# A fused adaLN attention and gated-MLP block: one chunk's output projection in two parts, one more quad off ScalarE, order constants anew

## The chip, the cores and the metric

One core of a Trainium2 chip runs the whole kernel in one launch. The metric is the device time of that launch in microseconds. The kernel before takes 805.92 us (median of three runs, 805.61 to 806.03).

Five engines run side by side, each through its own instruction stream, in order: PE (TensorE, matmuls), DVE (VectorE), ACT (ScalarE), POOL (GpSimd) and SP (SyncE, which here issues nearly all DMAs). They meet through semaphores.

## What is computed

```python
def _A_ref(x, wqkv, wo):                      # B, S, D = 1, 2048, 640; 32 heads of 20
    qkv = (x @ wqkv).reshape(B, S, 3, H, Dh).transpose(2, 0, 3, 1, 4)
    q, k, v = qkv
    p = softmax(einsum('bhqd,bhkd->bhqk', q, k) * Dh ** -0.5)
    o = einsum('bhqk,bhkd->bhqd', p, v)
    return o.transpose(0, 2, 1, 3).reshape(B, S, D) @ wo

def _B_ref(x, w_gate, w_up, w_down):          # F = 1536
    return ((x @ w_gate) * (x @ w_up)) @ w_down

sa, ca, ga, sb, cb, gb = (silu(c) @ w_mod).reshape(1, 6, 1, 640)   # six vectors
x = x + ga * _A_ref(layernorm(x) * (1 + ca) + sa, A_wqkv, A_wo)
x = x + gb * _B_ref(layernorm(x) * (1 + cb) + sb, B_w_gate, B_w_up, B_w_down)
```

All arrays are bf16. The layer norms have no weights of their own.

## The kernel before

**Tiling.** The 2048 query rows are cut into five chunks (`CHUNKS`): three of 512 rows and two of 256. The 32 heads are eight sets of four, numbered 0 to 7; the four heads of a set lie in the four 32-row strips of the PE array. An *item* is one head set of one chunk, 40 in all, and they run one after the other. For an item the scores of all 2048 keys are computed in units of 512 columns (one key tile by 512 queries, or two key tiles by 256 queries), 64 units in an item of the first three chunks and 32 in one of the last two.

**Two ways to the exponential.** Most units go in pairs into two PSUM banks, and ACT takes the exponential of 128x1024 in one instruction (line 1530). There are two such pairs of banks, used in turn, so a pair's next score matmuls wait until ACT has read it. The other units go to DVE in *quads* of four units: line 1554 turns each unit's scores into 16-bit integers in a buffer `DB`, lines 1586 and 1594 split their bits into a mantissa and an exponent part, and a product of the two parts (line 1591 on DVE, or four pieces at line 1646 on POOL) gives a first term; the exponent part is the second term. Both are multiplied with V, so a unit in a quad takes two PV matmuls where one on ACT takes one. `QUADS` gives the number of quads of each item, 109 in all.

**PV and the end of an item.** `pv_issue` (line 2179) multiplies the probabilities with V, accumulating in one PSUM bank. At the end of an item (`item_end_tasks`) DVE transposes the sums to `OT` (t1, line 1724), takes reciprocals of the row sums (t2, line 1728), POOL scales (t3, line 1730), DVE transposes back into one of two `OcT` buffers (t4, line 1738), and SP copies the rows with small DMAs into `Ocp` (line 1751), in which the rows of all heads lie packed as the output projection needs them. For set 7 of the last chunk alone (`direct`) there is no such DMA: the last row block of `Ocp` is zeroed at that chunk's set 0 (`z_tail`, line 1719), and the projection adds a sixth pass that reads `OcT` itself against `wo7`, a copy of the last 80 rows of `wo` laid out in the strips of `OcT`.

**After a chunk.** `suffix(ci)` makes the work that follows: the rows of x are loaded into `xck` by one DMA (line 1857); 8 rounds (4 row tiles by 2 column halves of 320; 4 rounds in the last two chunks) project `Ocp` with `wo` in five passes of 128 rows, and DVE adds x in `xck` (line 1878); statistics (1892, 1894, 1895, 1897) and the normalization into `xn2` (1900); transposes to `h2T` (1914, 1921); 12 blocks of gate and up with weights that SP streams into `stg`, or `stx` for the last two chunks (lines 951 and 947 on PE); the down projection from `hprod`; and the store. All chunks but the last do this while the next chunk's attention runs, in the places that the scores leave free on PE. Each round has a *gate*: it may not start before a number of exponentials have been issued. The last chunk's suffix comes after the last exponential, together with what is left of the fourth chunk's.

**What sets the order.** Nothing is reordered on the chip. At build time a planner (`Sched`) plays through all tasks with costs in nanoseconds, priorities and gates, and writes down the order on each engine; `emit_program` then adds the semaphore waits. On PE, `pick_pe` takes the next score matmuls when their banks are free, with up to two units of a quad attached; otherwise it takes PV work, or a round of the projections, or, where recent activity is low and nothing else is ready, a *zero fill* (`zero_fill`, line 2546: four matmuls that add zero into the PV bank). How it chooses depends on some fifteen constants, which `STAGE` sets for each item: how early a quad's units may be attached (`EAGER`) or must be (`D_LATE`, `D_RES`), how late scores may become through other work (`X_LATE`, `PVTOL`, `HOLD`), how much PV work is taken at once, from what activity on to fill (`FILL_MIN`, `FILL_Z`), and priorities of the products.

**Rounds and banks.** A `Round` is a group of matmuls into one PSUM bank with an evacuation. Rounds and quads' units share three banks (`G`). A round's first matmul waits for all its inputs, and since PE is in order, so does everything behind it. The out-projection of a chunk before the last waits for all DMAs into `Ocp` of its eight sets (`oc_ready`).

Of the kernel before, what the change touches and what calls it, by code (L numbers as in the profile page):

```python
# [329 lines left out]
def emit_program(nc, sched, nsem_dma=56):  # L330
# [97 lines left out]
    with nc.Block() as block:  # L428
# [20 lines left out]
        def _(e):  # L449
# [10 lines left out]
HALF = [0, 0, 4, 0, 0]  # L460
RESID, RES_G = 1, -20
D_LEAD = 0.451
# [80 lines left out]
    3: {"STEAL_GAP": 200, "PVMAX": 5, "FILL_MIN": 3892.39, "PVTOL": 199, "XBACK": 3, "D_RES": 11, "EAGER": 7, "D_LATE": 10},  # L543
    4: {"XBACK": 1, "PVMAX": 9, "EAGER": 3, "PVTOL": 324, "D_RES": 23, "Z_LATE": 272.45, "FILL_Z": 3546.61},
    5: {"EAGER": 7, "D_RES": 18, "PVCAP": 6, "FILL_MIN": 3318.38, "PVMIN": 1, "PVTOL": 124, "HOLD": 185, "FILL_Z": 4642.7, "D_LATE": 22, "STEAL_GAP": 244.44},
    6: {"PVCAP": 12, "FILL_MIN": 4293.4, "D_LATE": 12, "PVMIN": 5, "EAGER": 9, "TPRIO": 0.87, "HOLD": 80, "XDPRIO": 2.63, "FILL_Z": 3011.56},
    7: {"DL": 0.501, "PVTOL": 347, "D_LATE": 18, "HOLD": 155, "PVMAX": 9, "EAGER": 4, "X_LATE": 18.5},
    8: {"PVCAP": 15, "PVMAX": 3, "Z_LATE": 19.94, "FILL_Z": 3656.07, "FILL_MIN": 4663.83, "TPRIO": 0.57, "EAGER": 16, "PVMIN": 1, "XBACK": 3, "STEAL_GAP": 194.45, "XDPRIO": 2.05},
    9: {"X_LATE": -14.35, "PVCAP": 12, "XBACK": 0, "HOLD": 65, "PVMIN": 3, "D_LATE": 24, "PVMAX": 6, "D_RES": 23, "FILL_MIN": 4103.55, "XDPRIO": 1.63, "PVTOL": 224},
    10: {"PVMAX": 9, "X_LATE": -27.967, "EAGER": 5, "D_LATE": 15, "PVCAP": 8, "XBACK": 0, "HOLD": 110, "FILL_Z": 3693.44, "Z_LATE": -95.95, "PVMIN": 2, "XDPRIO": 1.25, "PVTOL": 199, "D_RES": 17},  # L550
    11: {"DL": 0.443, "X_LATE": 54.31, "FILL_MIN": 4086.76, "PVTOL": 270, "PVMAX": 6, "PVCAP": 14, "D_LATE": 22, "Z_LATE": -74.79, "EAGER": 4},
    12: {"DL": 0.459, "D_LATE": 11, "STEAL_GAP": 194.93, "X_LATE": -138.337, "HOLD": 125, "FILL_Z": 3256.59, "PVMIN": 1, "D_RES": 29},
    13: {"DL": 0.417, "D_RES": 4, "HOLD": 99, "PVMAX": 4, "TPRIO": 0.51, "PVMIN": 5, "STEAL_GAP": 145.61, "PVCAP": 13, "FILL_MIN": 5235.75, "FILL_Z": 2424.75, "PVTOL": 324, "Z_LATE": -67.84, "XDPRIO": 1.14},
    14: {"D_LATE": 14, "D_RES": 16, "FILL_MIN": 4279.59, "EAGER": 11, "X_LATE": -150.94, "STEAL_GAP": 200, "PVTOL": 374, "FILL_Z": 3396.29, "HOLD": 50, "XDPRIO": 1.59, "PVMAX": 10, "TPRIO": 1.17, "PVCAP": 9},
    15: {"X_LATE": -189.21, "EAGER": 15, "Z_LATE": -100, "D_RES": 5, "HOLD": 65, "PVMAX": 4, "PVMIN": 4, "PVTOL": 199, "STEAL_GAP": 191.33, "D_LATE": 14},
    16: {"D_RES": 67, "HOLD": 88, "PVCAP": 11, "PVMIN": 3, "PVTOL": 299, "STEAL_GAP": 83.35, "EAGER": 7, "Z_LATE": 121.81, "FILL_MIN": 4640.79, "FILL_Z": 2909.17, "D_LATE": 20, "X_LATE": 34.41, "PVMAX": 8, "XBACK": 1},
    17: {"D_LATE": 23, "PVMAX": 10, "PVMIN": 5, "FILL_MIN": 4231.45, "EAGER": 4, "FILL_Z": 3806.89, "PVCAP": 9, "XBACK": 4, "Z_LATE": 101.76, "TPRIO": 1.29, "HOLD": 80},
# [37 lines left out]
def build_kernel(nc, A_x, A_wqkv, A_wo, B_x, B_w_gate, B_w_up, B_w_down, c, w_mod, out):  # L595
# [195 lines left out]
    def dve(dur, f, deps=(), prio=3.0, **k):  # L791
        return sc.add(Task("dve", dur, f, deps, prio=prio, **k))
# [1829 lines left out]
```

## Time and profile before

| | |
|---|---|
| median of three runs | 805.92 us |
| the profiled execution | 805.69 us |
| its span, first to last instruction | 803.8 us |
| first exponential (line 1530) starts | 15.9 us |
| last exponential starts | 765.9 us |
| exponentials | 806 |
| quads (lines 1586 and 1594 each) | 109 |
| zero fills (line 2546) | 328 matmuls, in sets of four |
| products on POOL (line 1646) and on DVE (line 1591) | 264 pieces, 43 whole |

The page of the profile gives busy time, the span in 40 slices, the chain of work that ended last, and groups of instructions: line, engine, operation, output<-input, shapes, count | busy us, mean ns of one | idle time of the engine before them, and what ended it. A view of windows gives each engine's busy time (and instruction count) in a stretch, then the granted clock of PE, the DMA share and GB/s. A view of waits gives the waiting instruction, what it waited for, us in total, times and the longest. The timeline gives start, length, engine, line, operation and count; in it a run of matmuls ends with the modelled end of its last one, so that its neighbour's start tells more. For one line there is a view with the minimum, median and maximum duration, and the first and last start.

The output projection of the third chunk (512 rows, items 16 to 23) starts at 587.0 us on PE, and the first score matmuls of the fourth chunk at 575.5 us.

### The profile page before, as it was taken

How to read it: one execution, taken by the hardware profiler on the slowest of the kernel's cores; microseconds unless marked ns; L12 is line 12 of the kernel's file. 1: busy time of each engine (PE TensorE's matmuls, PEld its weight loads, DVE VectorE, ACT ScalarE, POOL GpSimd, SP SyncE). 2: the span in 40 equal slices, each digit the busy share in tenths (PEclk: the TensorE clock that was granted, in tenths of full speed). 3: DMA queues.
4: the chain of work that ended last, by engine and by line, in shares of the span. 5: the costliest groups of instructions: out<-in, count | busy, mean ns of one | idle time of the engine just before them, and what ended most of it. 6: DMA issues, size and time to landing. Idle time of an engine off the chain costs nothing.

```text
span 803.8 us, 29783 instructions
## 1 busy us (share of the span) xinstructions
PE 790.9 (98%) x12801; PEld 306.6 (38%) x12801; DVE 693.3 (86%) x1283; ACT 762.1 (95%) x851; POOL 364.1 (45%) x370
## 2 busy tenths in 40 slices
PE   8999999999999999999999999999999999999998
PEld 4433333222233223233233333333245544454577
DVE  7979977999989899989998999999689867978963
ACT  7899999999999999999999999999999999999922
POOL 3303266365665452156456553454475435443610
PEclk9999999999999999999999999999999999999999
DMA  9634211114330225000301221000303353004110
GB/s 311 208 87 109 68 46 40 44 37 126 87 73 23 58 66 173 18 15 23 95 7 24 54 56 34 5 23 23 87 9 71 82 131 86 13 24 105 31 38 17
DMA packets 108577, 52.80 MB, mean 66 GB/s; under 512 B 76043, under 2 KB 108447, under 8 KB 108447
## 3 DMA queue, kind: packets, MB, share of 16 engines
q1 hardware_dynamic: 107519, 49.75, 23.6%
q8 instruction: 102, 1.67, 0.9%
q10 hardware_dynamic: 928, 1.15, 0.4%
q14 instruction: 28, 0.23, 0.1%
HBM read 39.88 MB, written 8.41 MB: 60 GB/s over the span
## 4 chain that ended last, share of the span: by engine, by line
PE 61%; ACT 31%; DVE 4%; issue 3%; DMA 1%; ACTq 0%; DVEq 0%
ACT PP L1530 30%; PE ps_all L1492 20%; PE ps_all L951 20%; PE ps_all L2179 14%; PE ps_all L947 3%; DVE DB L1554 1%; PE ps_all L2546 1%; PE ps_all L1211 1%; DMA wm<-in_w_mod_dram 1%; PE ps_all L1914 1%; PE ps_all L1147 1%; PE ps_all L1108 1%; DVE wd L1475 1%; DVE DSS L1586 0%; DVE DSS L1594 0%
## 5 line engine op out<-in xcount | busy, mean ns | idle before, releaser
L1530 ACT ACTIVATE PP<-ps_all 128x1024 bf16<-128x1024 f32 x806 | 742.2, 1136 | 3.9 <-PE ps_all L1492 3.0
L1646 POOL TENSOR_TENSOR DSS<-DB,DSS 128x512 bf16<-128x512 bf16 x264 | 300.3, 1158 | 321.7 <-DVE DSS L1594 275.1
L1554 DVE TENSOR_SCALAR DB<-ps_all 128x512 int16<-128x512 f32 x436 | 290.3, 683 | 57.5 <-PE ps_all L1492 54.5
L1492 PE MATMUL ps_all<-QT,KT 32*128 32x512 bf16 (+1 forms) x2560 | 314.0, 340 | 7.1 <-ACT PP L1530 4.9
L1492 PEld LDWEIGHTS ps_all<-QT,KT 32*128 32x128 bf16 x2560 | 81.7, 91 | 263.2 <-ACT PP L1530 224.6
L2179 PE MATMUL ps_all<-PP,Vf 128*32 128x512 bf16 (+1 forms) x2024 | 159.1, 344 | 0.0
L951 PE MATMUL ps_all<-h2T,stg 128*32 128x512 bf16 (+2 forms) x1912 | 117.7, 329 | 0.0
L2179 PE MATMUL ps_all<-DSS,Vf 128*32 128x512 bf16 (+3 forms) x1072 | 85.1, 343 | 0.3 <-DVE DSS L1594 0.2
L1594 DVE TENSOR_SCALAR DSS<-DB 128x2048 int16<-128x2048 int16 x109 | 77.5, 711 | 1.3 <-PE ps_all L2179 1.2
L1586 DVE TENSOR_SCALAR DSS<-DB 128x2048 int16<-128x2048 int16 x109 | 74.9, 687 | 0.3
L2179 PEld LDWEIGHTS ps_all<-PP,Vf 128*32 128x32 bf16 x2024 | 44.6, 94 | 80.3 <-issue 75.3
L1730 POOL TENSOR_TENSOR OTn<-OT,invT 128x512 bf16<-128x512 f32 (+1 forms) x39 | 37.2, 953 | 53.5 <-DVE invT L1728 53.5
L951 PE MATMUL ps_all<-wd,hprod 128*32 128x320 bf16 (+1 forms) x1332 | 60.1, 283 | 0.2 <-DVE xck L2060 0.2
L951 PEld LDWEIGHTS ps_all<-h2T,stg 128*32 128x32 bf16 x1912 | 41.4, 95 | 31.1 <-issue 22.2
L1591 DVE TENSOR_TENSOR DSS<-DB,DSS 128x2048 bf16<-128x2048 bf16 x43 | 53.1, 1236 | 0.1
L951 PEld LDWEIGHTS ps_all<-wd,hprod 128*32 128x32 bf16 x1332 | 29.3, 96 | 19.3 <-issue 11.5
L2179 PEld LDWEIGHTS ps_all<-DSS,Vf 128*32 128x32 bf16 (+1 forms) x1072 | 26.6, 95 | 20.8 <-issue 11.9
L951 PE MATMUL ps_all<-wV,hT 128*32 128x320 bf16 (+1 forms) x696 | 32.5, 290 | 0.0
L1211 PE MATMUL ps_all<-hT,wq 128*32 128x512 bf16 x375 | 31.4, 383 | 0.2
L951 PE MATMUL ps_all<-wo,Ocp 128*32 128x320 bf16 (+1 forms) x660 | 29.9, 281 | 0.1
L2546 PE MATMUL ps_all<-ident 128*32 128x512 bf16 x328 | 29.0, 383 | 0.0
L1724 DVE STREAM_TRANSPOSE OT<-ps_all 128x512 f32<-128x512 f32 (+1 forms) x40 | 24.1, 603 | 5.3 <-PE ps_all L2179 5.3
(130 smaller groups left out, 529.8 us busy)
## 6 DMA issues: line engine op xcount, KB each, us to landing
stg<-in_B_w_gate_dram SPq DMA_DIRECT2D x44, 160.0 KB, 3.9
stg<-in_B_w_up_dram SPq DMA_DIRECT2D x44, 160.0 KB
QT<-q_rows SPq DMA_DIRECT2D x22, 128.0 KB, 2.5
KT<-k_rows SPq DMA_DIRECT2D x84, 32.0 KB, 2.9
wm<-in_w_mod_dram SPq DMA_DIRECT2D x3, 800.0 KB
x<-in_A_x_dram SPq DMA_DIRECT2D x7, 320.0 KB
xck<-in_A_x_dram SPq DMA_DIRECT2D x3, 640.0 KB, 4.6
wd<-in_B_w_down_dram SPq DMA_DIRECT2D x1, 1920.0 KB
```

What stands on the lines that cost most here:

```text
L951: return lambda e, b: e.matmul(ps[32 * x:32 * x + 32, b, c0 + o:c0 + o + w], lhs()[:, 32 * x:32 * x + 32], rhs() if w == n else rhs()[:, o ...
L1211: f = [lambda e, b_, k=k, x=x: e.matmul(ps[x:x + min(32, w - x), b_, :], wx[:, k, r0 + x:r0 + min(x + 32, w)], hT[tc][:, k, :], tile_posit ...
L1492: ems.append(lambda e, i=i, kt=kt: e.matmul(dstf()[:, i * u.n:(i + 1) * u.n], KT[32 * u.s:32 * u.s + 32, u.j, kt * 128:(kt + 1) * 128], QT ...
L1530: return e.activation(PPs[g % 2][:, cellp["p"], 0:nu * 512], ps[:, b0:b0 + nu, :].rearrange("p b c -> p (b c)"), AFT.Exp, scale=ESCALE)
L1554: return e.tensor_scalar(DBl[st_["slot"]][:, x * 512:(x + 1) * 512], bank(cell["b"]), EBIAS, 0.0, op0=ALU.add, op1=ALU.max)
L1586: return e.tensor_scalar(DSl[st_["ss"][0]][:, :], DBl[st_["slot"]][:, :], 0x7F, 0x3F00, op0=ALU.bitwise_and, op1=ALU.bitwise_or)
L1591: return e.tensor_tensor(d, DBl[st_["slot"]][:, :].bitcast(BF16), d, ALU.mult)
L1594: return e.tensor_scalar(DSl[st_["ss"][1]][:, :], DBl[st_["slot"]][:, :], 0x7F80, 2, op0=ALU.bitwise_and, op1=ALU.bitwise_or)
L1646: return e.tensor_tensor(d, DBl[st_["slot"]][:, x * w:x * w + w].bitcast(BF16), d, ALU.mult)
L1730: f3 = lambda e: e.tensor_tensor(OTn[:, 0:n].rearrange("p (b c r) -> p b r c", c=32, r=2), OT[:, 0:n].rearrange("p (b r c) -> p b r c", c= ...
L2179: ems.append(lambda e, i=i, kt=kt, stt=stt, stp=stp: e.matmul(ps[32 * s:32 * s + mc, BPV, 0:u.n], Vf[:, (kt * H + 4 * u.j + s) * VW:(kt * ...
L2546: task.emits = [lambda e, x=x: e.matmul(ps[32 * x:32 * x + 32, b_, :].rearrange("p (a b) -> p a b", a=4), ident[:, 32 * x:32 * x + 32], id ...
```

## The change

`QUADS` gets one quad more, in set 6 of the fourth chunk: 110.

For the third chunk (`OPA_C = (2,)`) set 7 is now `direct` as in the last chunk: no DMAs into `Ocp`, and the row block is zeroed at that chunk's set 0. Its out-projection is made in two parts. Eight rounds `oa` take the five passes over `Ocp` without waiting for set 7, with a gate 30 exponentials before the next chunk, and their evacuation adds x and writes an fp32 buffer `pf`. Eight rounds `op` then take the one pass over `OcT` with `wo7`, and their evacuation adds `pf` and writes `xck`. `pf` lies where `h2T` and `xn2` lie; so the evacuations into it wait for the chunk before to be done with `h2T`, and the normalization into `xn2` waits for the second part's evacuations of tiles 2 and 3. x is loaded a tile at a time, each tile after the store of that tile of the chunk before. Priorities on DVE and POOL are given for these tasks (`OPA_P`, `OPB_P`, `OPL_P`, `OPX_P`).

The constants in `STAGE` are replaced for 36 of the 40 items (3 to 10 and 12 to 39).

```diff
-         (1, 2, 1, 2, 2, 1, 1, 2),
+         (1, 2, 1, 2, 2, 1, 2, 2),
          (1, 2, 2, 1, 3, 0, 2, 2))
 HALF = [0, 0, 4, 0, 0]
 RESID, RES_G = 1, -20
+OPA_C, OPA_G, OPB_G, OPA_P, OPB_P, OPL_P, OPX_P = (2,), -30, 0, 0.7, 0.6, 0.6, 0.6
...
-    3: {"STEAL_GAP": 200, "PVMAX": 5, "FILL_MIN": 3892.39, "PVTOL": 199, "XBACK": 3, "D_RES": 11, "EAGER": 7, "D_LATE": 10},
+    3: {"STEAL_GAP": 200, "PVMAX": 5, "FILL_MIN": 3892.39, "PVTOL": 199, "XBACK": 3, "D_RES": 11, "EAGER": 6, "D_LATE": 10},
...
-    22: {"PVMAX": 4, "FILL_MIN": 2500, "D_RES": 17, "EAGER": 6, "D_LATE": 14, "PVCAP": 10, "PVTOL": 224, "STEAL_GAP": 189.38, "FILL_Z": 4191.54, "HOLD": 200, "X_LATE": -70.46, "PVMIN": 4},
+    22: {"PVMAX": 4, "FILL_MIN": 2500, "D_RES": 11, "EAGER": 6, "PVCAP": 13, "PVTOL": 224, "STEAL_GAP": 189.38, "FILL_Z": 4191.54, "HOLD": 260, "PVMIN": 4, "X_LATE": -4.54},
...
+    pf_off = [R2.off]
     h2T = R2.alloc("h2T", [128, KD, 512], BF16)
     xck = R2.alloc("xck", [128, 4, D], BF16)
+    pf_off.append(R2.off)
     xn2 = R2.alloc("xn2", [128, 4, D], BF16)
+    pf = [at("pf", [128, 2, D], F32, o) for o in pf_off]
...
-        direct = j == NSET - 1 and ci == NC - 1
+        direct = j == NSET - 1 and (ci == NC - 1 or ci in OPA_C)
+        if direct and ci != NC - 1:
+            t2.prio = t4.prio = OPA_P
...
+        nx_ = 1 if ci in OPA_C else ntl
+        d_xc = dma("sp", 128 * nx_ * D * 2, lambda e: e.dma_start(xck[:, 0:nx_, :], xv[:, t0:t0 + nx_, :]),
+                   (first if alt else bd["out"][:1] if ci in OPA_C else bd.get("out", []) + v_last), prio=15, gate=max(0, gb + XC_G))
...
+        for tl in range(ntl if opa else 0):
+            for hf in range(2):
+                mms = [(C320, quarters(320, lambda k=k, tl=tl: Ocp[:, slot, k, tl * 128:(tl + 1) * 128],
+                                       lambda k=k, hf=hf: wo_sb[:, k, 320 * hf:320 * hf + 320], k == 0, k == KD - 1))
+                       for k in range(KD)]
+                def after(r, tl=tl, hf=hf):
+                    f = lambda e: e.tensor_tensor(pf[tl // 2][:, tl % 2, 320 * hf:320 * hf + 320], ps[:, r.b["b"], 0:320],
+                                                  xck[:, tl, 320 * hf:320 * hf + 320], ALU.add)
+                    return [dve(ps_cost(320), f, [r.last, d_xt[tl]] + bd["h2T"] + bd["tr"], prio=1)]
+                r = Round(mms, oc_ready[ci][:-1] + t_wo + [d_xt[tl]], after, pbase - 600 + 2 * tl + hf, gate=max(0, gb + OPA_G),
+                          name=f"oa{ci}.{tl}")
...
+        for tl in range(ntl if opa else 0):
+            for hf in range(2):
+                mms = [(C320, quarters(320, lambda tl=tl: OcT[:, oc_last[ci]["s"], tl * 128:(tl + 1) * 128],
+                                       lambda hf=hf: wo7[:, 320 * hf:320 * hf + 320], True, True))]
+                def after(r, tl=tl, hf=hf):
+                    f = lambda e: e.tensor_tensor(xck[:, tl, 320 * hf:320 * hf + 320], ps[:, r.b["b"], 0:320],
+                                                  pf[tl // 2][:, tl % 2, 320 * hf:320 * hf + 320], ALU.add)
+                    return [dve(ps_cost(320), f, [r.last, ev_a[(tl, hf)]], prio=OPB_P)]
+                r = Round(mms, [oc_ready[ci][-1]] + t_wo, after, pr(True), gate=max(0, gb + OPB_G), name=f"op{ci}.{tl}")
...
+        if opa:
+            first = first + [ev_b[(tl, hf)] for tl in (2, 3) for hf in range(2)]
```

More of the change, by code (lines that the diff above doesn't have):

```diff
@@ L546 @@
[L546 to L549, printed above, removed]
@@ L1856, in pr @@
             return pbase + rc_[0] - (1500 if tail and early else OPFIRST if early else 0)
-        d_xc = dma("sp", 128 * ntl * D * 2, lambda e: e.dma_start(xck[:, 0:ntl, :], xv[:, t0:t0 + ntl, :]),
-                   (first if alt else bd.get("out", []) + v_last), prio=15, gate=max(0, gb + XC_G))
+        nx_ = 1 if ci in OPA_C else ntl
+        d_xc = dma("sp", 128 * nx_ * D * 2, lambda e: e.dma_start(xck[:, 0:nx_, :], xv[:, t0:t0 + nx_, :]),
+                   (first if alt else bd["out"][:1] if ci in OPA_C else bd.get("out", []) + v_last), prio=15, gate=max(0, gb + XC_G))
+        d_xt = [d_xc] * ntl
+        if ci in OPA_C:
+            d_xt = [d_xc] + [dma("sp", 128 * D * 2, lambda e, tl=tl: e.dma_start(xck[:, tl, :], xv[:, t0 + tl, :]),
+                                 [bd["out"][tl]], prio=15, gate=max(0, gb + XC_G)) for tl in range(1, ntl)]
         t_xn2 = []
@@ L1888, in suffix @@
                 op_last.append(r.last)
+            if opa:
+                ev = [ev_b[(tl, hf)] for hf in range(2)]
             t = t0 + tl
+            lp = LN2T if tail else OPL_P if opa else LN2P
             bn = []
```

95 lines of the change are left out of this document (57 added, 38 removed).

## The prediction

> **What bounds the kernel now.** I began with the page: busy shares, the slices and the chain that ended last.
>
> ```profile
> span 803.8 us, 29783 instructions
> PE 790.9 (98%) x12801; PEld 306.6 (38%) x12801; DVE 693.3 (86%) x1283; ACT 762.1 (95%) x851; POOL 364.1 (45%) x370
> PE   8999999999999999999999999999999999999998
> DVE  7979977999989899989998999999689867978963
> ACT  7899999999999999999999999999999999999922
> PEclk9999999999999999999999999999999999999999
> PE 61%; ACT 31%; DVE 4%; issue 3%; DMA 1%; ACTq 0%; DVEq 0%
> ```
>
> ACT is full until slice 38 and then nearly idle; PE is full throughout. The chain goes back and forth between them: an exponential needs its score matmuls, and score matmuls need the PSUM pair that an earlier exponential releases. The groups and the waits say which of the two the other waits for.
>
> ```profile
> L1530 ACT ACTIVATE PP<-ps_all 128x1024 bf16<-128x1024 f32 x806 | 742.2, 1136 | 3.9 <-PE ps_all L1492 3.0
> L1646 POOL TENSOR_TENSOR DSS<-DB,DSS 128x512 bf16<-128x512 bf16 x264 | 300.3, 1158 | 321.7 <-DVE DSS L1594 275.1
> L1554 DVE TENSOR_SCALAR DB<-ps_all 128x512 int16<-128x512 f32 x436 | 290.3, 683 | 57.5 <-PE ps_all L1492 54.5
> L1594 DVE TENSOR_SCALAR DSS<-DB 128x2048 int16<-128x2048 int16 x109 | 77.5, 711 | 1.3 <-PE ps_all L2179 1.2
> L1586 DVE TENSOR_SCALAR DSS<-DB 128x2048 int16<-128x2048 int16 x109 | 74.9, 687 | 0.3
> L1591 DVE TENSOR_TENSOR DSS<-DB,DSS 128x2048 bf16<-128x2048 bf16 x43 | 53.1, 1236 | 0.1
> PEld ps_all L1492 <- ACT PP L1530: 224.6, 623, 0.8
> ```
>
> ACT idled 3.9 us ahead of 806 exponentials, while PE's score loads stood 224.6 us waiting for ACT, 623 times. So up to the last exponential ACT sets the pace, and PE fills its slots of one exponential each with whatever is there, zero fills (L2546) included. The pace, in two stretches, and the fills in two:
>
> ```profile
> core 0: us, PE busy (x) PEld busy (x) DVE busy (x) ACT busy (x) POOL busy (x), PEclk, DMA share, GB/s
> 100.00:576.00 476.00, 469.16 (x6617) 147.79 (x6619) 430.38 (x729) 475.53 (x520) 242.78 (x225) 1.00 0.20 52
> 576.00:767.00 191.00, 189.87 (x4228) 92.05 (x4224) 157.70 (x311) 190.86 (x207) 93.59 (x97) 1.00 0.25 58
> ...
> 540.00:600.00 60.00, 11.98 (x136) 2.91 (x136) 1.00 0.17 40
> 600.00:767.00 167.00, 1.81 (x20) 0.44 (x20) 1.00 0.28 65
> ```
>
> (The last two rows are of L2546 alone, PE and PEld.) Exponentials follow each other every 475.53/520 = 0.914 us in the first three chunks and every 190.86/207 = 0.922 us in the last two. 136 of the 328 fills stand between 540 and 600 us, where the third chunk's out-projection is still waiting for its eighth head set; after 600 us there are 20. The timeline of PE, where it changes over to the end:
>
> ```profile
> 564.77 0.61 PE L2546 MATMUL ps_all<-ident 128*32 128x512 bf16 x8
> 567.75 0.39 PE L2546 MATMUL ps_all<-ident 128*32 128x512 bf16 x4
> ...
> 765.43 0.39 PE L1492 MATMUL ps_all<-QT,KT 32*128 32x256 bf16 x4
> 767.18 0.40 PE L2179 MATMUL ps_all<-PP,Vf 128*32 128x256 bf16 x8
> 767.39 0.83 PE L951 MATMUL ps_all<-h2Tt,stx 128*32 128x256 bf16 x24
> 768.05 2.36 PE L951 MATMUL ps_all<-h2Tt,stg 128*32 128x256 bf16 x80
> 770.34 1.12 PE L947 MATMUL ps_all<-wo,Ocp 128*128 128x320 bf16 x7
> 774.06 3.44 PE L951 MATMUL ps_all<-wd,hprodt 128*32 128x320 bf16 x96
> 777.44 0.73 PE L1914 MATMUL ps_all<-ident,xn2c 128*128 128x128 bf16 x10
> ```
>
> After the last score matmul (765.43) PE runs without a pause to the end. The end is therefore the time of the last score, which ACT's pace sets, plus the PE work that stands behind it. A set of four fills takes 0.61 - 0.39 = 0.22 us from start to start; a 256-wide matmul 2.29/80 = 0.029 us (768.05 to 770.34); a 320-wide one 3.38/96 = 0.035 us; eight 256-wide PV matmuls 0.21 us (767.18 to 767.39).
>
> **The change part by part.** *The 110th quad.* It takes four units of 512 columns from ACT in the fourth chunk's set 6; an exponential does two, so 806 become 804. At the pace of its stretch that is 2 x 0.922 = 1.84 us less; at the first stretch's pace 1.83. The row's mean duration, 1.136 us, is no price, since neighbours overlap: 806 x 1.136 would be 916 us, and the busy time is 742.2. (The Trainium skill, Perfetto Trace Analysis, "Per-instruction lifecycle", has ACT's window run on to the acknowledgement of the write, after the next instruction can have begun; by that window the two would be 2.27 us and the sum 0.43 us lower. The trace sides with the spacing.)
>
> For the quad DVE gets 4 x 0.67 (290.3/436) + 0.71 + 0.69 = 4.1 us, PE eight more 256-wide PV matmuls (0.21 us). The order of the changed kernel also moves three quads' products from POOL to DVE, net of the new one: four more on DVE, 4 x 1.24 = 4.9 us, twelve fewer pieces on POOL, 12 x 1.16 = 13.9 us. One more memset of Ocp on POOL takes 0.53 us:
>
> ```profile
> L1719 POOL MEMSET Ocp<- x1: 525/525/525, 604.0 to 604.0; 128x512 bf16 x1
> L1878 DVE TENSOR_TENSOR xck<-ps_all,xck x24: 435/482/492, 230.5 to 602.3; 128x320 bf16<-128x320 f32 x24
> L1751 SPq DMA_DIRECT2D Ocp<-OcT x176: 554/712/1887, 78.2 to 767.8; - x176
> L1857 SPq DMA_DIRECT2D xck<-in_A_x_dram x3: 396/428/915, 195.7 to 560.9; - x3
> xck<-in_A_x_dram SPq DMA_DIRECT2D x3, 640.0 KB, 4.6
> SPq L1857 <- DMA out_dram<-xck: 1.7, 1, 1.7
> ```
>
> *The out-projection in two parts.* Part one is the old rounds with the eighth set's rows of Ocp zeroed; part two is 8 rounds of one more pass over OcT and wo7: 32 matmuls of 320, 32 x 0.035 = 1.1 us more on PE. Eight more evacuations on DVE, 8 x 0.48 = 3.9 us. An evacuation with an fp32 buffer as its output (part one) or its second input (part two) is in no row. From below it costs what a matmul evacuation with bf16 does, 0.48 us; from above I take the 128x512 evacuation's 0.68 (L1554), for 16 of them 16 x 0.20 = 3.2 us more. I take the lower: same shape, same PSUM source. Four Ocp DMAs fall away on SP (4 x 0.71 us), and one load of x becomes four, a tile each (L1864, L1868 of the changed kernel; 3 x 0.43 us more). DVE gets 12.9 us in all. That lies beside ACT: DVE idles 476 - 430.4 = 45.6 us in the first stretch and 33.3 in the second; without that cover it would be 12.9 us on the path. PE's 1.3 us are covered by fills: the order has 236 matmuls of a fill's kind for 336 before, 25 sets or 5.5 us fewer. Those behind score matmul 1480 fall from 160 to 92.
>
> *What moves.* In the order, the out-projection's first matmul comes behind score matmul 1515 instead of 1608, its second part begins behind 1586 and ends behind 1602 instead of 1684; the transposes to h2T behind 1636 instead of 1684. For that its set 6 must be normalized and copied earlier: that set's reciprocal on DVE now stands right behind its OT transpose. The up-projection of that chunk still ends behind score matmul 2116, as before, so most of the lead is spread out over later slots and not carried to the end. Counted along PE's records of before, score matmul 1515 is in the first of these rows and 1586 in the second; the third is the old projection's beginning, so the lead is about 21 us:
>
> ```profile
> 565.45 0.40 PE L1492 MATMUL ps_all<-QT,KT 32*128 32x512 bf16 x4
> 583.70 0.39 PE L1492 MATMUL ps_all<-QT,KT 32*128 32x256 bf16 x4 [0.20 <-ACT PP L1530]
> 587.00 0.32 PE L951 MATMUL ps_all<-wo,Ocp 128*32 128x320 bf16 x4
> ```
>
> *The end.* Behind the last score matmul the old order has 140 matmuls of the fourth chunk's up-projection and 24 of PV, the new one 120 full ones, four half ones and 16. That is 18 x 0.029 + 0.21 = 0.72 us less. From there both orders agree to the last row.
>
> *The order constants.* 36 of 40 stages have new constants; on PE the order differs from the fourth head set on, some 727 exponentials. One nanosecond of their mean spacing is 0.73 us. Counted from the two orders with the spacings above, slots that hold over 0.55 us of work besides scores and fills are 49 of 714 before and 53 of 712 after; the mean work between scores 1602 and 2550 falls from 0.454 to 0.436 us a slot. I price the replanning at nothing, and between -2 and +2 ns a slot, a quarter of the 8 ns by which the two stretches differ: -1.4 to +1.4 us.
>
> *Sum.* The profiled execution took 805.69 us with a span of 803.8, so 1.9 us lie outside. The span becomes 803.8 - 1.84 - 0.72 = 801.2, the execution 803.1. The median of the runs is 0.23 us above the profiled one: 805.92 - 2.56 = 803.4 us.
>
> **The rivals.** *B, DVE gets behind at the second part.* In the new order eight part-two evacuations, eight statistics and four normalizations stand on DVE with a single L1554 between them, and PE's rounds wait, in order and ahead of score matmuls, for the three PSUM banks that these evacuations free.
>
> ```profile
> 576.00:600.00 24.00, 22.91 (x472) 10.01 (x464) 18.97 (x39) 24.00 (x27) 14.38 (x16) 1.00 0.03 9
> 600.00:624.00 24.00, 23.96 (x566) 12.79 (x566) 22.71 (x53) 23.92 (x27) 13.37 (x16) 1.00 0.26 60
> ```
>
> Against it: DVE has 5.0 us free in 576 to 600. For it: only 1.3 in the next 24 us. Were the whole 3.9 us of added evacuations to hold up the scores it would be 807.3; at half, 805.3.
>
> *C, slower: score matmuls come late to the exponentials.* The place is every replanned slot, in which PE, in order, runs over with other work before its score matmuls. The price is 0.73 us for each nanosecond. It eats the gain at 2.56/0.727 = 3.5 ns and makes the kernel slower by over 0.2% from (2.56 + 1.61)/0.727 = 5.7 ns. If the replanned slots became 8 ns longer, as the last stretch already is against the first, that is 5.8 us: 809.2. For it: 36 stages of new constants, and the slot counts say neither better nor worse. Against it: PE is less loaded in the last stretch.
>
> *D, it doesn't come ahead.* Part one's last tile needs its rows of x, whose load now stands on SP behind the copies of that chunk's set 6, while PE, in order, holds the next score matmuls behind that round. The load of all four tiles landed in 4.6 us, and SP waited 1.7 us for the store before it. Late by 0 to 4.6 us: 803.4 to 808.0, the middle 805.7.
>
> *E, the clock.* Fewer fills mean a less busy PE. A microsecond of PE's work at half the granted clock makes it late by half a microsecond of span, and past 2 x (2.56 + 1.61) = 8.3 us of span so spent the kernel is slower; 10 us give 803.4 + 5 = 808.4. Against it: every row above shows 1.00, and a slot of 0.92 us always holds score matmuls. (The Trainium skill, TensorE: Matmul & The Clock Gate, "Part 1: The HAM clock gate", halves the clock after an idle window of about 3.4 us; the trace of before, at 1.00 throughout, neither bears that out nor speaks against it.)
>
> **How the numbers follow.** The forecast has 0.58, B 0.20, C 0.14, D 0.06, E 0.02. A run can tell 0.2%, 1.6 us, from no change: faster is below 804.3, slower above 807.5. The forecast's own range is 803.4 - 1.4 to 803.4 + 1.4, 802.0 to 804.8, of which 0.53 are faster and 0.05 same; B gives 0.02 faster, 0.18 same; C 0.13 slower, 0.01 same; D 0.05 same, 0.01 slower; E half and half. Faster 0.55, same 0.30, slower 0.15. The range goes from 801.9 to 808.0, the ends of the forecast and of D, which leaves out most of C and a little below.
>
> **What would show it.** Right: 804 exponentials, spaced 0.91 and 0.92 us as now; 100 fills fewer, two thirds of them from about 555 us on; wo with Ocp on PE from about 566 us, with OcT from about 584; the last score matmul 1.8 us earlier and the rest 0.7 us shorter. B would show as PE waiting on DVE at the pf evacuations and ACT idle at about 585 to 600; C as ACT's spacing up by some nanoseconds in many stages, with idle time put to PE L1492; D as a gap on PE with a DMA of x as its end; E as a PEclk below 1.00. The prediction is wrong if the exponentials' spacing changes by more than 2 ns, whatever the out-projection does.

## The result, and the profile after

The changed kernel takes 803.63 us (median of nine runs, 803.46 to 803.76); the kernel before, in nine runs, 805.71 (805.61 to 806.03). The ratio is 0.9973, with a 95% interval of 0.9963 to 0.9983: 2.1 us faster. The forecast was 803.4.

The profiled execution took 803.48 us, 2.21 less than that of before, and its span is 2.1 us shorter. The page of the changed kernel, whose lines answer to those of before:

```profile
span 801.7 us, 29815 instructions
PE 787.4 (98%) x12817; PEld 306.7 (38%) x12817; DVE 704.7 (88%) x1301; ACT 760.3 (95%) x849; POOL 352.6 (44%) x359
ACT  7899999999999999999999999999999999999922
PE 50%; ACT 40%; issue 5%; DVE 3%; DMA 1%; ACTq 0%; DVEq 0%
...
L1534 ACT ACTIVATE PP<-ps_all 128x1024 bf16<-128x1024 f32 x804 | 740.3, 1133 | 4.1 <-PE ps_all L1496 3.1
L1650 POOL TENSOR_TENSOR DSS<-DB,DSS 128x512 bf16<-128x512 bf16 x252 | 286.7, 1159 | 322.3 <-DVE DSS L1598 266.9
L1558 DVE TENSOR_SCALAR DB<-ps_all 128x512 int16<-128x512 f32 x440 | 293.4, 683 | 46.8 <-PE ps_all L1496 45.2
```

Two exponentials fewer, four more units on DVE, twelve fewer pieces on POOL, and ACT idles as little ahead of its exponentials as before (4.1 us for 3.9) and is full until the same slice. The chain that ended last goes through ACT for 40% of the span, for 31% before. DVE's busy time is up by 11.4 us (12.9 had been reckoned), of which nothing shows at the end. The first exponential starts at 15.90 us in both traces, the last at 764.22 us for 765.89 (1.67 earlier), so the mean spacing is 748.32/803 = 0.9319 us for 749.99/805 = 0.9317: two tenths of a nanosecond apart. That mean hides two shifts. The first exponential of the fourth chunk, the 601st, starts 0.32 us earlier (575.57 for 575.89), so the spacing up to there fell from 0.9333 to 0.9328 us; from there to the last it rose, from 0.9269 to 0.9293 us (188.65/203 for 190.00/205). From the last exponential's start to the end it is 37.46 us for 37.93 (0.47 less). Together that is the 2.1 us.

The windows of the same stretches, the two around the second part, and the identity fills alone (here L2600, PE and PEld):

```profile
core 0: us, PE busy (x) PEld busy (x) DVE busy (x) ACT busy (x) POOL busy (x), PEclk, DMA share, GB/s
100.00:576.00 476.00, 468.10 (x6731) 149.66 (x6729) 435.78 (x737) 475.66 (x520) 231.13 (x214) 1.00 0.20 52
576.00:767.00 191.00, 189.35 (x4209) 92.35 (x4206) 165.37 (x327) 188.92 (x204) 93.78 (x97) 1.00 0.25 58
...
576.00:600.00 24.00, 23.39 (x455) 10.25 (x450) 22.33 (x55) 24.00 (x27) 12.35 (x17) 1.00 0.01 3
600.00:624.00 24.00, 23.24 (x541) 12.15 (x542) 22.83 (x47) 23.90 (x27) 13.56 (x12) 1.00 0.33 75
...
540.00:600.00 60.00, 5.16 (x56) 1.38 (x56) 1.00 0.15 38
600.00:767.00 167.00, 2.21 (x24) 0.55 (x24) 1.00 0.28 66
```

Between 540 and 600 us 136 identity fills have become 56. DVE is busy for 22.33 of the 24 us in which the second part stands, for 18.97 before, and ACT for all 24.00: it was not held up. (The fills of these rows, L2546 before, put an identity product into a spare bank. The zero fills proper, into the PV bank, stand in a line of their own, 8 matmuls before and 12 after.)

PE's timeline at the two parts and behind the last score matmul, and the two kinds of evacuation with the new fp32 buffer (minimum, median and maximum in ns, first and last start):

```profile
565.65 0.32 PE L955 MATMUL ps_all<-wo,Ocp 128*32 128x320 bf16 x4
...
582.79 0.64 PE L955 MATMUL ps_all<-wo,OcT 128*32 128x320 bf16 x8
...
763.78 0.39 PE L1496 MATMUL ps_all<-QT,KT 32*128 32x256 bf16 x4
764.10 0.41 PE L2233 MATMUL ps_all<-PP,Vf 128*32 128x256 bf16 x8
764.33 1.33 PE L955 MATMUL ps_all<-h2Tt,stx 128*32 128x128 bf16 x44
765.47 0.29 PE L955 MATMUL ps_all<-h2Tt,stg 128*32 128x256 bf16 x4
765.58 0.40 PE L2233 MATMUL ps_all<-PP,Vf 128*32 128x256 bf16 x8
765.80 0.40 PE L2233 MATMUL ps_all<-DSS,Vf 128*32 128x256 bf16 x8
766.02 2.25 PE L955 MATMUL ps_all<-h2Tt,stg 128*32 128x256 bf16 x76
```

```profile
L1883 DVE TENSOR_TENSOR pf<-ps_all,xck x8: 429/480/493, 569.8 to 582.6; 128x320 f32<-128x320 f32 x8
L1896 DVE TENSOR_TENSOR xck<-ps_all,pf x8: 474/480/490, 583.6 to 586.8; 128x320 bf16<-128x320 f32 x8
```

The first part starts at 565.65 us and the second at 582.79, without idle time ahead of either. Behind the last score matmul stand 24 PV matmuls (8 at 764.10, 8 at 765.58, 8 at 765.80), as many as before.

### The profile page after: what moved, and what is told of

The parts are those of the page before. It is cut to its first block, busy times and chain, and to the rows that moved or that the text cites. A ratio compares the mean times of both kernels' runs of the same rounds, so it can differ in the third digit from the quotient of the medians.

```text
span 801.7 us, 29815 instructions
## 1 busy us (share of the span) xinstructions
PE 787.4 (98%) x12817; PEld 306.7 (38%) x12817; DVE 704.7 (88%) x1301; ACT 760.3 (95%) x849; POOL 352.6 (44%) x359
## 3 DMA queue, kind: packets, MB, share of 16 engines
q8 instruction: 102, 1.67, 0.9%
## 4 chain that ended last, share of the span: by engine, by line
PE 50%; ACT 40%; issue 5%; DVE 3%; DMA 1%; ACTq 0%; DVEq 0%
ACT PP L1534 40%; PE ps_all L1496 16%; PE ps_all L955 14%; PE ps_all L2233 11%; PE ps_all L1215 3%; PE ps_all L951 3%; PE ps_all L1151 2%; DVE DB L1558 1%; DMA wm<-in_w_mod_dram 1%; PE ps_all L1112 1%; DVE DSS L1590 1%; PE ps_all L976 0%; DVE DSS L1598 0%; DVE DSS L1595 0%; PE ps_all L1968 0%
## 5 line engine op out<-in xcount | busy, mean ns | idle before, releaser
L1650 POOL TENSOR_TENSOR DSS<-DB,DSS 128x512 bf16<-128x512 bf16 x252 | 286.7, 1159 | 322.3 <-DVE DSS L1598 266.9
L1558 DVE TENSOR_SCALAR DB<-ps_all 128x512 int16<-128x512 f32 x440 | 293.4, 683 | 46.8 <-PE ps_all L1496 45.2
L2233 PE MATMUL ps_all<-PP,Vf 128*32 128x512 bf16 (+1 forms) x2016 | 158.0, 344 | 0.1
L955 PE MATMUL ps_all<-h2T,stg 128*32 128x512 bf16 (+2 forms) x1936 | 119.4, 327 | 1.0 <-DVE DB L1558 0.8
L2233 PE MATMUL ps_all<-DSS,Vf 128*32 128x512 bf16 (+2 forms) x1088 | 85.0, 341 | 0.0
L2233 PEld LDWEIGHTS ps_all<-PP,Vf 128*32 128x32 bf16 x2016 | 44.9, 94 | 78.9 <-issue 73.4
L955 PE MATMUL ps_all<-wd,hprod 128*32 128x320 bf16 (+1 forms) x1380 | 61.9, 279 | 0.0
L1595 DVE TENSOR_TENSOR DSS<-DB,DSS 128x2048 bf16<-128x2048 bf16 x47 | 59.8, 1272 | 0.1
L2233 PEld LDWEIGHTS ps_all<-DSS,Vf 128*32 128x32 bf16 x1088 | 27.6, 95 | 18.3 <-issue 8.6
L2091 DVE TENSOR_TENSOR hprod<-ps_all,gsb 128x512 bf16<-128x512 f32 x32 | 21.7, 679 | 4.3 <-PE ps_all L955 4.3
```

The source lines that it names most:

```text
L955: return lambda e, b: e.matmul(ps[32 * x:32 * x + 32, b, c0 + o:c0 + o + w], lhs()[:, 32 * x:32 * x + 32], rhs() if w == n else rhs()[:, o ...
L1558: return e.tensor_scalar(DBl[st_["slot"]][:, x * 512:(x + 1) * 512], bank(cell["b"]), EBIAS, 0.0, op0=ALU.add, op1=ALU.max)
L1595: return e.tensor_tensor(d, DBl[st_["slot"]][:, :].bitcast(BF16), d, ALU.mult)
L1650: return e.tensor_tensor(d, DBl[st_["slot"]][:, x * w:x * w + w].bitcast(BF16), d, ALU.mult)
L2233: ems.append(lambda e, i=i, kt=kt, stt=stt, stp=stp: e.matmul(ps[32 * s:32 * s + mc, BPV, 0:u.n], Vf[:, (kt * H + 4 * u.j + s) * VW:(kt * ...
```

## The experiments

In the table, "long slots" is worked out from the order on PE, not from a trace: the work besides scores and fills that a slot between two exponentials holds beyond 0.7 us, summed over all slots. "ACT idle" is the idle time ahead of the exponentials in the group's row. "Last" is the start of the last exponential, "tail" from there to the end of the span. The kernel before took 805.7 to 805.8 us beside each.

| kernel | us | ratio, 95% interval | last | tail | ACT idle | long slots |
|---|---|---|---|---|---|---|
| before | 805.71 | | 765.89 | 37.93 | 3.9 | 0.1 |
| changed | 803.63 | 0.9963 to 0.9983 | 764.22 | 37.46 | 4.1 | 0.1 |
| e1 quad alone | 808.79 | 1.0026 to 1.0054 | 765.82 | 40.87 | 5.0 | 0.6 |
| e2 two parts alone | 817.92 | 1.0137 to 1.0165 | 777.93 | 37.93 | 15.3 | 8.7 |
| e3 constants alone | 817.58 | 1.0132 to 1.0160 | 776.11* | 40.22 | 13.2* | 6.9 |
| e4 quad and constants | 813.29 | 1.0077 to 1.0105 | 773.50* | 37.46 | 12.3* | 6.5 |
| e5 two parts and constants | 808.55 | 1.0028 to 1.0057 | 771.70* | 39.35 | 6.8* | 0.7 |
| e6 four units left out | 807.16 | 1.0008 to 1.0025 | 764.23 | 41.09 | 4.0 | 0.1 |
| e12 one constant moved | 810.74 | 1.0051 to 1.0079 | 771.15* | 39.09* | 11.5* | 6.9 |

(* "Last", "tail" and "ACT idle" are of the profiled execution, and four of these are not plain. That of e5 took 812.84 us, with some 4 us lost in the first item, where its granted clock is 0.66 between 20 and 30 us; the other five took 808.53 to 808.62. That of e12 took 812.03 us, the other three 810.72 to 810.75. In e3 and e4 the clock fell in the second chunk, as shown below.)

**The parts of the change, one at a time.** e1 is the kernel before with the new row of `QUADS`; e2 the changed kernel with the old constants and the old `QUADS`; e3 the changed kernel with `OPA_C = ()` and the old `QUADS`, which leaves the constants.

```diff
 e1, against before:
-         (1, 2, 1, 2, 2, 1, 1, 2),
+         (1, 2, 1, 2, 2, 1, 2, 2),
 e3 and e4, against changed (e3 with the old QUADS too):
-OPA_C, OPA_G, OPB_G, OPA_P, OPB_P, OPL_P, OPX_P = (2,), -30, 0, 0.7, 0.6, 0.6, 0.6
+OPA_C, OPA_G, OPB_G, OPA_P, OPB_P, OPL_P, OPX_P = (), -30, 0, 0.7, 0.6, 0.6, 0.6
 e5, against changed (e2 too, with the old STAGE):
-         (1, 2, 1, 2, 2, 1, 2, 2),
+         (1, 2, 1, 2, 2, 1, 1, 2),
```

> The kernel before with the 110th quad alone: old constants, out-projection in one part. By its order 804 exponentials, and behind the last score matmul 212 matmuls of the fourth chunk's up-projection where before has 140. Theory (the end is the last score, at ACT's pace, plus what PE still has behind it): -2 x 0.922 + 72 x 0.029 = +0.2 us, so about 805.9 and no change. Rival (the quad is worth its two exponentials whatever else): 803.9.

> The out-projection in two parts alone: 109 quads, old constants. By its order 806 exponentials, 140 matmuls left behind the last score, as before, though the projection starts behind score matmul 1542 instead of 1608. Theory: no change, 805.7 within 0.7. Rival (moving the projection into the filled stretch is the gain, 5.5 us of fills saved): 801 to 804.

> The new constants alone: 109 quads, one part. By its order 806 exponentials and 174 matmuls left behind the last score (before 140): theory +34 x 0.029 = +1.0 us, 806.7. Rival (the constants are the gain): about 803.6.

> The quad and the new constants without the out-projection in two parts. By its order 804 exponentials and 122 matmuls left (before 140, the change 122). Theory: -1.84 - 0.52 = -2.4 us against before, 803.3, level with the change within 0.7. Rival (the two parts make the room that the quad needs): 805 to 806.

No part gains alone, and each misses what was expected of it by 2.9 us or more. The quad alone removes two exponentials and yet the last one starts only 0.07 us earlier, and the tail grows by 2.9 us: its order has 212 up-projection matmuls behind the last score for 140, which is 72 x 0.029 = 2.1 us. e2 to e4 show something else, a few long stalls, and in e3 and e4 a fall of the clock besides. ACT's timeline in e2, and PE's in the same stretch:

```profile
607.66 4.90 ACT L1534 ACTIVATE PP<-ps_all 128x1024 bf16<-128x1024 f32 x5
620.07 6.52 ACT L1534 ACTIVATE PP<-ps_all 128x1024 bf16<-128x1024 f32 x7 [7.50 <-PE ps_all L2233]
```

```profile
612.62 0.39 PE L1496 MATMUL ps_all<-QT,KT 32*128 32x256 bf16 x4
...
614.62 3.46 PE L955 MATMUL ps_all<-h2T,stg 128*32 128x256 bf16 x120 [0.46 <-DVE h2T L1975]
...
619.61 0.94 PE L2233 MATMUL ps_all<-PP,Vf 128*32 128x256 bf16 x26 [0.40 <-DVE OT L1728]
...
621.15 0.41 PE L1496 MATMUL ps_all<-QT,KT 32*128 32x256 bf16 x8
```

The planner has put 120 gate and up matmuls in one piece (3.4 us), and transposes with short waits for DVE, ahead of the PV work that frees the probabilities' buffer. So ACT stands for 7.50 us, and of the score matmuls none starts between those at 612.62 and those at 621.15. The exponentials' rows say the same of e3 and e4, whose idle time ended on PV (L2233) for half:

```profile
L1534 ACT ACTIVATE PP<-ps_all 128x1024 bf16<-128x1024 f32 x806 | 743.0, 1136 | 13.2 <-PE ps_all L1496 6.5 <-PE ps_all L2233 6.4
```

```profile
L1534 ACT ACTIVATE PP<-ps_all 128x1024 bf16<-128x1024 f32 x804 | 741.4, 1130 | 12.3 <-PE ps_all L2233 6.4 <-PE ps_all L1496 5.4
```

The longest of these stalls are written into the order, since the column of long slots, taken from the orders alone, has them: 6.5 to 8.7 us for 0.1. In e3 and e4 a part is the clock's. The windows 260 to 265 and 265 to 272 us of e3, and then of e4:

```profile
260.00:265.00 5.00, 3.79 (x37) 1.68 (x34) 5.00 (x11) 5.00 (x7) 3.01 (x3) 1.00 0.22 64
265.00:272.00 7.00, 6.91 (x56) 2.03 (x56) 4.27 (x8) 4.59 (x6) 1.05 (x1) 0.51 0.05 12
```

```profile
260.00:265.00 5.00, 3.92 (x33) 1.61 (x33) 5.00 (x10) 5.00 (x6) 2.39 (x3) 1.00 0.23 66
265.00:272.00 7.00, 6.63 (x74) 2.29 (x77) 4.59 (x9) 4.95 (x6) 1.05 (x1) 0.76 0.04 11
```

ACT stands for 2.4 of the 7 us in e3 and 2.1 in e4, against losses of 11.7 and 7.5 us in all. How much of that the order alone would have cost is not separated.

**Without the quad, and without the work that it takes from ACT.** e5 is the changed kernel without the quad. e6 is the kernel before with four units of set 6 of the fourth chunk left out altogether (scores, exponentials and PV; its output lacks them).

> The change without its 110th quad (two parts and new constants stay). 806 exponentials; by its order one slot holds 1.33 us of work besides scores (the change has none above 0.9), 150 matmuls of the up-projection are left behind the last score (the change 122) and 8 PV matmuls fewer. Theory (last score at ACT's pace, plus what PE has behind it): 803.6 + 1.84 + 28 x 0.029 - 0.21 + about 0.8 for the long slot = 806.8. Rival (two parts and constants are the gain, the quad adds nothing): 803.6 to 804.3.

> The kernel before, with the four units that the 110th quad would take left out altogether (a part of the keys of set 6 of the fourth chunk is not computed): 804 exponentials, and nothing added on DVE or PE. Its order has no slot above 0.9 us, as before, but 228 matmuls left behind the last score instead of 140. Theory (in the old program PE is as full as ACT, so that time taken from ACT comes back behind the last score): -1.84 + 88 x 0.029 to 88 x 0.041 (the rate of the quad alone), 806.4 to 807.5. Rival (ACT alone is the bound): 803.9.

e5 is 4.9 us slower than the changed kernel, 1.7 more than the theory allowed; the rival missed by more. Taken at its face the quad is worth more than its two exponentials there, though e1 shows it worth less than nothing in the old order; but the order of e5 has a stall of 1.34 us on PV at 742 us that the changed kernel has not, so this is not the quad's price. e6 went as expected: two exponentials are gone, the last starts 1.66 us earlier, nearly all that ACT can give, and the kernel is 1.4 us slower than before. The time is back behind the last score, where 228 up-projection matmuls stand for 140 (88 x 0.029 = 2.6 us). Less room for PE's work in two slots fewer is one part of that. The order was planned anew as well: when each PE matmul is counted from its start to the next one's, from the fourth chunk's first exponential to the end, e6 spends 0.57 us less on scores, 0.86 more on fills (three sets) and 0.9 more in waits.

**Which engine is full.** Three kernels have the order of before on every engine, so that nothing is replanned. e8 makes every fourth exponential of the last two chunks 64 columns wide instead of 1024 (PV then reads what an earlier one left). e9 halves the columns that the third chunk's gate and up matmuls write (the rest of the bank keeps what stood there). e10 does both. (The expectations name 51 of 204 exponentials, the up-projection and 61,400 columns. The edits cut 52 of 206 exponentials, and half of those columns, in gate and up together; the 12.8 us are right for that.)

```diff
 e8:
         def fexp(e, nu=nu, b0=b0, cellp=cellp, g=g):
+            if g >= gstart[3] and g % 4 == 0:
+                return e.activation(PPs[g % 2][:, cellp["p"], 0:64], ps[:, b0, 0:64], AFT.Exp, scale=ESCALE)
 e9, in a copy of the helper for the rounds of the third chunk's gate and up (abridged):
-            return lambda e, b: e.matmul(ps[32 * x:32 * x + 32, b, c0 + o:c0 + o + w], lhs()[:, 32 * x:32 * x + 32],
+            return lambda e, b: e.matmul(ps[32 * x:32 * x + 32, b, c0 + o:c0 + o + w // 2], lhs()[:, 32 * x:32 * x + 32],
```

> The kernel before in its own order, with every fourth exponential of the last two chunks (51 of 204) cut from 1024 to 64 columns (the rest of its output is stale). If ACT alone sets the pace, each saves about 0.8 us: 805.8 - 41 = 765. If PE stands right behind it, little is saved: PE idles about 1 us in 576 to 767, so 798 to 805.

> The kernel before, same order on every engine, every instruction kept; only the third chunk's up-projection matmuls write half of their columns (so that chunk's output is not the reference's). That is about 61,400 columns of TensorE, 12.8 us at the row's rate of 0.0268 us for 64 columns of four quarters, taken out between 606.6 and 684 us, ScalarE's work untouched. Theory now (TensorE and ScalarE are both full there): exponentials can come no closer than the 0.904 us that they have where nothing holds them up; the 83 of that stretch stand at 0.928, so 83 x 0.024 = 2.0 us less at the most: 803.7 to 805.0, and the tail as before. Rival, TensorE alone sets the pace of the last two chunks: 805.7 - 12.8 = 793. Rival, the prediction's (ScalarE alone): 803.7 to 805.7 too, so that this run tells only against TensorE alone, and the next one is needed. If the clock is taken back with less work, above 805.7.

> The kernel before, same order, with both cuts at once: half the columns of the third chunk's up-projection (12.8 us of TensorE between 606.6 and 684 us) and every fourth exponential of the last two chunks on 64 columns (some 0.68 us of ScalarE each by the busy time that the short exponentials alone saved, 14 us of it between 606.6 and 684). Alone the short exponentials gave 1.1 us. Theory now (both are full): the two together give far more than the sum of the two alone, 9 to 13 us in 606 to 684 and 1 in 576 to 588: 792 to 796. Rival, a third resource (VectorE's evacuations, or the order's own handshakes between the score banks) sets the pace: the sum of the two alone, 802.5 to 804. If the clock is taken back, in between, with PEclk below 1.00.

| | us | ratio, 95% interval | less than before |
|---|---|---|---|
| e8, ACT relieved | 804.60 | 0.9977 to 0.9995 | 1.1 |
| e9, PE relieved | 804.53 | 0.9976 to 0.9994 | 1.2 |
| e10, both | 798.94 | 0.9902 to 0.9929 | 6.7 |

The stretch 600 to 700 us in the windows of before, e8, e9 and e10, in this order:

```profile
600.00:700.00 100.00, 99.97 (x2152) 46.84 (x2150) 82.90 (x163) 99.92 (x109) 46.46 (x49) 1.00 0.33 75
```

```profile
600.00:700.00 100.00, 99.97 (x2152) 46.86 (x2152) 82.47 (x161) 81.88 (x109) 47.09 (x50) 1.00 0.33 76
```

```profile
600.00:700.00 100.00, 93.26 (x2178) 45.13 (x2174) 83.67 (x164) 99.94 (x110) 47.53 (x50) 1.00 0.33 76
```

```profile
600.00:700.00 100.00, 96.08 (x2281) 47.70 (x2278) 87.52 (x170) 85.45 (x115) 49.95 (x52) 1.00 0.34 77
```

Before, PE is busy for 99.97 us of the 100 and ACT for 99.92. With 18 us taken off ACT, PE stays at 99.97 and no more than the 109 instructions of before fit on ACT. With PE's idle time at 6.7 us, ACT stays at 99.94 and it is 110. With both it is 115. So neither engine alone is the bound of this stretch; either one is enough to hold the pace.

The size for e10 was expected too large: some 10 to 14 us, for 6.7. It is not that the halved matmuls save little: by the starts of the single records, four quarters of 128 columns stand 0.056 us behind the four before them, where four of 256 columns take 0.109 (within a four the starts are 0.002 to 0.009 us apart). The 12.8 us of columns did come out, though PE's busy time fell by 6.7 only: a record of 128 columns lasts 0.219 us up to its modelled end, so that a short pause behind it counts as busy. With both engines relieved neither is full any more (96.08 and 85.45 us of 100), and ACT's idle time ahead of its full exponentials ends on score matmuls, for 31.5 of 32.6 us in the whole run. So a third limit seems to have a part in e10, perhaps the handshake between the two pairs of score banks that the expectation named; no run separates it.

**The fills.** e7 is the changed kernel with every fill behind the first 20 us cut from 512 columns to 8, in the same order (fills add nothing to the result). The diff shows the identity fills; the zero fills are cut likewise.

```diff
-                ps[32 * x:32 * x + 32, b_, :].rearrange("p (a b) -> p a b", a=4), ident[:, 32 * x:32 * x + 32], idb,
+                ps[32 * x:32 * x + 32, b_, 0:8], ident[:, 32 * x:32 * x + 32], ident[:, 0:8],
```

> The change with each fill matmul behind the first 20 us cut from 512 to 8 columns, everything else in the same order. Theory (fills stand where PE would be idle, and the clock needs none of them): 803.6 within 0.3, clock 1.00. Rival (the clock): a granted clock below 1.00 between 540 and 600 us and 805 or more.

It takes 818.89 us (ratio 1.0158 to 1.0184), 15 us more than the changed kernel. The clock in 40 slices of the run, and some windows, say why:

```profile
PEclk9999999999988999999886999999879999999999
...
565.00:570.00 5.00, 4.73 (x83) 1.68 (x81) 4.43 (x9) 5.00 (x7) 1.05 (x1) 1.00 0.01 3
570.00:575.00 5.00, 3.83 (x52) 1.16 (x52) 3.41 (x8) 5.00 (x7) 4.49 (x4) 0.92 0.14 45
575.00:580.00 5.00, 5.00 (x50) 1.32 (x52) 3.50 (x5) 4.08 (x5) 0.00 (x0) 0.50 0.96 206
580.00:585.00 5.00, 5.00 (x86) 1.73 (x79) 3.65 (x7) 4.38 (x6) 2.49 (x3) 0.89 0.16 31
...
605.00:620.00 15.00, 15.00 (x262) 6.58 (x266) 12.16 (x26) 12.69 (x15) 5.36 (x7) 0.66 0.13 29
620.00:767.00 147.00, 145.41 (x3234) 69.97 (x3226) 127.07 (x241) 146.70 (x160) 71.20 (x72) 1.00 0.30 71
```

In a window the last figure but two is the granted clock. Between 570 and 575 us PE was busy for 3.83 of 5 us, and in the next 5 us the clock is 0.50: 50 matmuls take all of the 5.00 us, and ACT has time left over. Later it is down again, 0.66 over 15 us; from 620 us on, where fills are few, it is 1.00. It had been down in the second and third chunks too; the mean over the run is 0.964. A busy share of 77% is no threshold: in e2, at a clock of 1.00 throughout, PE was busy for 3.88 of 5 us from 617.8 us on.

**Two more orders.** e12 is the changed kernel with one constant of one stage moved (`"HOLD": 260` to `250` in stage 22). e11 is the changed kernel with a 111th quad, in set 7 of the last chunk.

> The changed kernel with one constant of one stage moved by a little, HOLD of stage 22 from 260 to 250; no instruction is added or taken away, the planner only puts them in another order from there on (out-projection from score matmul 1546 instead of 1515, 78 zero and identity fills more). Slots that hold over 0.7 us of work besides scores: 6.9 us in excess, for 0.1 in the changed kernel. Theory now (the constants fit one program only, and long slots cost 1.2 to 1.4 us for each counted): 811 to 814. Rival, the prediction's price of a replanning (at most 2 ns a slot): 802.2 to 805.

> The changed kernel with a 111th quad, in set 7 of the last chunk: 802 exponentials, an order without long slots, 140 up-projection matmuls and 48 of PV behind the last score instead of 122 and 24. By the prediction's way of counting: 2 x 0.92 less for two exponentials, (18 + 24) x 0.029 = 1.2 us more behind the last score: 803.6 - 0.6 = 803.0. Theory now: a quad alone gives nothing where TensorE is full and its work comes back behind the last score: 803.6 to 805, and the last exponential starts no more than 1.2 us earlier than in the changed kernel.

e12 takes 810.74 us, 7.1 more than the changed kernel (its profiled execution 8.6 more). Beside the order itself, some 76 more fills and two quads' products (on POOL instead of DVE) are all that differs. Its exponentials' row shows ACT idle for 11.5 us, 7.4 more, and most of it ends on PV again:

```profile
L1534 ACT ACTIVATE PP<-ps_all 128x1024 bf16<-128x1024 f32 x804 | 739.8, 1143 | 11.5 <-PE ps_all L2233 7.2 <-PE ps_all L1496 4.1
```

e11 takes 805.48 us (ratio 0.9988 to 1.0005), the same as before and 1.9 more than the changed kernel. The last exponential starts at 762.27 us, 1.95 earlier than in the changed kernel, which is more than the 1.2 that the second theory allowed; the last score matmul is 1.24 us earlier (762.54 for 763.78). What stands behind that one is 3.2 us longer (41.16 for 37.92). Counted, it is 42 matmuls, 1.2 us; another 1.3 us are waits that the changed kernel does not have there, one of them for the product of a quad; 0.7 us stays open:

```profile
771.20 0.63 PE L2229 MATMUL ps_all<-DSS,Vf 128*32 128x256 bf16 x16 [0.28 <-POOL DSS L1646]
...
779.67 0.73 PE L1964 MATMUL ps_all<-ident,xn2c 128*128 128x128 bf16 x10 [0.19 <-DVE xn2c L1950]
781.19 11.08 PE L947 MATMUL ps_all<-h2Tc,stx 128*128 128x256 bf16 x100 [0.79 <-ACT h2Tc L1973]
```

No complete kernel that was run beats the changed one.

## Why the prediction was right, point by point

**The time and the terms of the sum.** The last exponential was to start 1.84 us earlier and does so by 1.67; the rest was to be 0.72 us shorter and is so by 0.47. The second term was mis-sized by a miscount: behind the last score the new order has 24 PV matmuls, not 16, as the timeline shows. Without the 0.21 us for these the term is 18 x 0.029 = 0.52 us, and the gain 2.36 us, where 2.08 was measured. That the time itself comes out at 803.6 either way is partly luck: the sum started from 805.92, the median of three runs, where the median of the nine runs is 805.71.

**"Up to the last exponential ACT sets the pace."** For the last two chunks this is half of it. e8 took 35 us off ACT between 576 and 767 us (156.14 busy for 190.86) and gained 1.1; e9 and e10 show PE as the other half, for the third chunk's gate and up. The prediction read PE's loads waiting 224.6 us for ACT as PE having room. The waits are those of single loads, over the whole span; the room was in the fills, and after 600 us there were only 20. The spacings of 0.914 and 0.922 us that it took from the windows are a little low, since a window's count takes in instructions across its edges: by their starts exponentials stood 0.918 us apart from 100 to 576 us and 0.927 in the last two chunks. For two exponentials that makes 0.01 us.

**The price of the quad.** Of the 1.67 us, 0.32 were won before the fourth chunk begins. In the last two chunks, where the two exponentials fell away, it is 1.35 us and not 1.84, since the others there stand 2.4 ns further apart (0.5 us). And the price is not the quad's own. Where PE is full too, two exponentials fewer are two slots fewer, and some of PE's work falls behind the last score instead (e1, e6). The prediction had in hand what makes room for it and booked it elsewhere: it counted the fills that fall away, from 160 to 92 behind score matmul 1480, as cover for 1.3 us of new work on PE. They are 17 sets, 17 x 0.22 = 3.7 us, and the moved out-projection stands in their place. Less the 1.3 us PE has 2.4 us to give, near the 2.1 by which the span became shorter.

The two traces agree with this account. Count each PE matmul from its start to the next one's, from the 481st exponential (at 466 us) to PE's end: fills take 5.9 us less, the out-projection 2.0 more, the gate, up and down projections 1.7 more and the rest, waits included, 0.4 more, together about 1.8 less. From the fourth chunk's first exponential on, it is 1.8 less, with the out-projection, now partly done before it, down by 2.2. That is an account and no experiment, and it does not tell which edit brought what. What the runs show is that, in the orders that the planner made, the quad does not pay without the two parts (e1, e4), nor the two parts without the quad (e5). e4 and e5 differ from the changed kernel in their planned order as well, and e4 in its clock, so what either edit is worth by itself in a good order stays open; the quad and the two parts with the old constants were not run.

**The replanning at nothing, within 1.4 us.** For the changed kernel this held on the mean, to 0.2 ns a slot, but as a sum of two shifts: 0.3 us less up to the fourth chunk and 0.5 us more behind it. The 2.4 ns there exceed the 2 ns at which the prediction called itself wrong, so that the small mean is in part luck. As a bound for any replanning it fell: e2, e3, e4 and e12 lie 5 to 12 us above before. The rival in which score matmuls come late has the mechanism of these orders, in a few places of 2 to 8 us and not as some nanoseconds in every slot. The orders told which it would be: the excess of long slots is 0.1 us in both kernels and 6.5 to 8.7 in those four. The prediction counted slots above 0.55 us (49 and 53) and left it at "neither better nor worse"; the sum above a higher bound would have spoken against this rival beforehand.

**DVE behind at the second part.** It did not happen: the evacuations took 0.480 us at the median with either fp32 operand, the lower of the two bounds, and ACT was busy for 24.00 of 24 us. PE's loads waited 0.6 us in all for the first part's evacuations and 0.2 for the second's.

**The first part does not come ahead.** It did. The last load of x was issued at 563.9 us, the first round ran at 565.65 without a wait, the second part at 582.79, where 566 and 584 had been forecast.

**The clock.** It stayed at 1.00, but one of the reasons given was wrong: e7 has score matmuls in every slot too, and its clock fell to 0.50. What e7 shows is that the fills which were left, 56 of them between 540 and 600 us, were needed at their full width. That the out-projection stands in for the others that fell away is argued from the windows, not shown by a run. The Trainium skill, TensorE: Matmul & The Clock Gate, "Part 1: The HAM clock gate", puts the lower clock behind an idle window of about 3.4 us; in e7 it came behind 5 us in which PE was 77% busy, and PE's longest pause between 540 and 620 us was 0.41 us. So in this case the clock was lost without such a window.

## What to carry to other kernels

Where two engines are both full, price an edit in both accounts: time taken from one is worth little until the other loses some too (1.1 us for 35 us off ACT here), and filler on the second engine is the place to look for it. A planned order is part of the kernel: after any edit sum up the work in its longest slots before trusting a price per instruction, since one slot of 3 us costs more than the edit can bring. Try the parts of a change alone, but read a part's loss as that of its order first.

## What had not been expected of the hardware

The granted clock halved in e7 behind 5 us in which PE was 77% busy with scores and PV in every slot, and 15 us went by thinning work that computes nothing; in e3 and e4 it fell for a few microseconds with no fill thinned. And taking 12.8 us of columns off PE in e9 showed as only 6.7 us of idle time in the profile, so that PE's busy share understates what was freed.
